# Attention and maxout FFN: pairs 14 to 31 turned by transposing DMAs between SBUF tiles, three requests moved in the opening

## The chip, the cores and the metric

The kernel runs on one core of a Trainium2 chip, as one program in one launch. The metric is the device time of an execution in microseconds (us). Five engines work on their own lists of instructions and wait for one another by semaphores: PE (TensorE, matmuls and transposes; its weight loads are shown apart as PEld), DVE (VectorE), ACT (ScalarE), POOL (GpSimd) and SP (SyncE, which here only issues DMAs). Sixteen DMA engines move the data. All times from the trace are counted from the first instruction of the profiled execution.

## The reference, cut to what matters

Attention runs per batch b (8) and head h (8) over 576 queries of width 64, with 16 beacon keys and values put before the 576 ordinary ones. The beacons are seen by all queries; the rest is causal. The result, 4608 tokens of 512, goes through a feed-forward layer with three first matrices, of which the maximum is taken, and one last matrix.

```python
k_all = np.concatenate([beacon_k, k], axis=2)
v_all = np.concatenate([beacon_v, v], axis=2)
scores = scale * np.matmul(q, k_all.transpose(0, 1, 3, 2))
scores = np.where(causal, -1000000000.0, scores)
a = np.exp(scores - scores.max(-1, keepdims=True))
a /= a.sum(-1, keepdims=True) + 1e-09
attn_out = np.matmul(a, v_all)                       # [B, H, S, D]
x = attn_out.transpose(0, 2, 1, 3).reshape(B * S, H * D)
h = np.maximum(np.maximum(x @ w1, x @ w2), x @ w3)   # 4608 x 768
out = h @ w_out                                      # 4608 x 512
```

Inputs and output are float32; the kernel computes in bf16 with float32 sums.

## The kernel before

**Pairs.** Two heads of one batch make a pair: 32 pairs, four to a batch. Pair p works in query tile qT (128 partitions: two heads of 64, 576 columns) and key tile kT (592 columns: 16 beacons, 576 keys), of which there are six each (`NT`), used in turn: p % 6. Two pairs make a block (`quad` in the code), and the main loop (L1140) handles blocks 4 to 15, that is pairs 8 to 31. The first eight pairs run in an opening that is written out as a list of steps (`first_steps`, L892).

**What a block does.** Scores of the first pair (`emit_scores`, L506: PE multiplies kT by qT into PSUM, ACT takes the exponential into `at_sb`, L532); the product with the values for the block before (`emit_pv`, L571, L592), its normalization on ACT and DVE (L612 to L624); then the rest of the scores, with POOL masking the causal edge (`emit_masks`, L538, L551). Between these stand units of the feed-forward layer (`mm1_unit`, L643 and L654, with DVE keeping the running maximum in hT, L664; `mm2_unit`, L685 and L690, with DVE's copy to y, L702). How many units stand at each of the six places of a block is set by hand in `gaps` (L1084). Once the attention is finished, at some 245 us, only feed-forward units remain.

**How q and k come into qT and kT.** `load_pair` (L192) loads a pair's q and k into a float32 staging tile, 96 partitions with six consecutive rows each, so that one piece of a row in DRAM is 6 x 64 x 4 = 1536 bytes. There are eight staging tiles, shared with the values, and a load follows the cast that frees one. `cast_pair` (L254, L248) casts it into the bf16 tile p, on POOL or ACT, with both heads side by side: 96 partitions x 6 rows x 128. From there two ways lead on:

- Pairs 4 to 15 are turned by PE (`turn_pair`, L472): six transposes for q and six for k (L401) into one tile of a ring of three PSUM tiles, then a copy of the keys on DVE (L467) and of the queries on ACT (L456), which put the columns into order.
- Pairs 16 to 31 are stored to DRAM (`store_pair`, L371) and fetched from there with a transposing DMA (`fetch_pair`, L380, L382 and L383). Their beacons are stored next to the keys in DRAM (`open_dram`, L362), so that one fetch brings both.

The beacons of batches 0 to 3 are turned by PE into `bT` and copied by ACT or POOL into the first 16 columns of kT (`place_beacons`, L461, L463).

**What sets the order.** Each engine runs its list in the order in which the program emits it. All loads, stores and fetches of the loop are issued by SP, in order: `at_step` (L773, L1068 to L1081) hangs them on steps (pair, first or second half). Pair p is cast at step p-5, stored at p-4 and fetched at p-3. An instruction at the head of a queue that waits holds all behind it. A DMA also waits for the one eight places ahead of it in SP's queue, whose semaphore it reuses. In the opening, some loads are gated: a memset of a few elements on DVE or POOL (L198, L283, L332) writes the target first, and the DMA waits for it, which sets when it may start. `load_w_out` (L330) does so for the last matrix, through POOL's DMA queue.

Of the kernel before, what the change touches and what calls it, by code (L numbers as in the profile page):

```python
# [8 lines left out]
FP32 = mybir.dt.float32  # L9
BF16 = mybir.dt.bfloat16  # L10
# [6 lines left out]
def kernel(  # L17
# [46 lines left out]

    B_PE = 4


# [52 lines left out]
    pv_psum = ctx.enter_context(tc.tile_pool(name="pv_psum", bufs=1, space=PSUM))  # L120
    dram_pool = ctx.enter_context(tc.tile_pool(name="dram", bufs=B - B_PE, space=bass.MemoryType.DRAM))
    ffn_stack = ctx.enter_context(ExitStack())
# [6 lines left out]
    NB_DMA = Nb * (B - B_PE)  # L129
    bT = const.tile([128, PPB, NB_PE], BF16, name="bT")  # L130
    bk32_0 = const.tile([Nb, H, D], FP32, name="bk32_0")
# [60 lines left out]
    def load_pair(p, gate=None):  # L192
        b, g, j0 = place(p)
        hs = slice(head(g, j0), head(g, j0) + 2)
        st = new_stage(("pair", p))

        if gate:
            gate.memset(st[0:QP, 0:1], 0.0)  # L198
        for i, src in enumerate((q, k)):
            nc.sync.dma_start(  # L200
                out=st[0:QP, i * NQ2 : (i + 1) * NQ2].rearrange("p (h x) -> p h x", h=2),
                in_=src[b, hs].rearrange("h (p r) d -> p h (r d)", r=QR),
            )

# [153 lines left out]

    q_dram = {}
    k_dram = {}  # L360

    def open_dram(b):  # L362
        q_dram[b] = dram_pool.tile([PPB, S, 2 * D], BF16, name="q_dram")
        k_dram[b] = dram_pool.tile([PPB, NK, 2 * D], BF16, name="k_dram")
        lo = Nb * (b - B_PE)
        nc.sync.dma_start(
            out=k_dram[b][:, 0:Nb].rearrange("i n x -> n i x"),
            in_=bk16[lo : lo + Nb].rearrange("n (i h) d -> n i (h d)", h=2),
        )

    def store_pair(p):  # L371
        b, pi = divmod(p, PPB)
        for i, dst in enumerate((q_dram[b][pi], k_dram[b][pi, Nb:NK])):
            src = stage.pop(("pair16", p, i))
            nc.sync.dma_start(
                out=dst.rearrange("(p r) x -> p (r x)", r=QR),
                in_=src.rearrange("p r h d -> p (r h d)"),
            )

    def fetch_pair(p):  # L380
        b, pi = divmod(p, PPB)
        nc.sync.dma_start_transpose(out=qTs[p % NT], in_=q_dram[b][pi])  # L382
        nc.sync.dma_start_transpose(out=kTs[p % NT][:, 0:NK], in_=k_dram[b][pi])  # L383

# [383 lines left out]

    plan = {}

    def at_step(p, g, *fns):  # L773
        plan.setdefault((p, g), []).extend(fns)

    def load_v_pieces(b):
# [11 lines left out]
    def next_load(n=1, gate=None):  # L788
        for _ in range(n):
            if loads:  # L790
                loads.pop(0)(*([idle[gate]] if gate else []))

    def C(fn, *a):
        def run():
            fn(*a)
            next_load()

        return run

# [48 lines left out]
    def widen():  # L848
        ffn_stack.close()
        wide = ctx.enter_context(tc.tile_pool(name="wide_psum", bufs=1, space=PSUM))  # L850
        ring.append((wide, "wide"))

    by = {"dve": by_dve, "act": by_act, "pool": by_pool}
    queue = {"sp": nc.sync, "act": nc.scalar}
# [34 lines left out]
        "load": next_load,  # L889
        "store": lambda: store_y(len(y_out)),  # L890
    }
# [108 lines left out]
        ("scores", 5, 0, 1),  # L1000
        ("scores", 4, 0, 0),
        ("scores", 4, 3, 0),
        ("ffn", "pv", 1),
        ("ffn", "ring", 0),
        ("load pair", 8, "dve"),
        ("ffn", "pv", 1),
        ("scores", 5, 3, 0),
        ("mask", 5, 0, "dve"),
        ("mask", 4, 2, "dve"),
        ("mask", 5, 3, "dve"),  # L1010
        ("load pair", 9, "pool"),
        ("scores", 5, 2, 0),
# [16 lines left out]
        ("mask", 5, 1, "pool"),  # L1029
        ("scores", 6, 0, 0),  # L1030
        ("ffn", "pv", 1),
        ("load", 1),
# [3 lines left out]
        ("cast pair", 8),  # L1036
        ("load w_out", "dve"),
        ("whole", 7, "ring"),
# [28 lines left out]
    ]  # L1067
    for p in range(10, B_PE * PPB):  # L1068
        at_step(p - 2, 0, C(cast_pair, p, by_pool, by_pool))
    for b in range(2, B):  # L1070
        p = b * PPB
        at_step(p + 1, 0, C(cast_v, b, 0, by_pool))
        at_step(p + 1, 1, C(cast_v, b, 1, by_pool))
    at_step(B_PE * PPB - 6, 1, L(by_pool, bk16, bk32))
    for b in range(B_PE, B):
        p = b * PPB
        at_step(p - 4, 0, L(open_dram, b))
        for i in range(PPB):
            at_step(p + i - 5, 0, C(cast_pair, p + i, by_act if b < 6 else by_pool, by_pool))
            at_step(p + i - 4, 0, L(store_pair, p + i))  # L1080
            at_step(p + i - 3, 0, L(fetch_pair, p + i))  # L1081


    gaps = {  # L1084
        4: (3, 2, 2, 3, 2, 1),
        5: (3, 1, 1, 3, 1, 1),
        6: (3, 1, 2, 0, 2, 1),
        7: (5, 1, 1, 1, 1, 0),
        8: (2, 3, 2, 7, 0, 2),
        9: (5, 1, 1, 1, 2, 0),  # L1090
        10: (2, 1, 2, 5, 2, 1),
        11: (3, 1, 1, 1, 2, 0),
        12: (2, 1, 2, 9, 0, 1),
        13: (5, 1, 1, 1, 0, 2),
        14: (2, 1, 2, 9, 2, 0),
        15: (4, 2, 1, 5, 2, 5),
    }

    def emit_all():
        for name, *args in first_steps:  # L1100
            steps[name](*args)
        n_y = 0

        def run_plan(p, s):
            for fn in plan.pop((p, s), ()):
                fn()

        def stored():
            nonlocal n_y
            store_y(n_y)  # L1110
            n_y = len(y_out)

        v_tiles.pop(0)
        early_stack.close()
        y_pool.append(ctx.enter_context(tc.tile_pool(name="ffn_y", bufs=4)))

        def singles(n):
            for _ in range(n):
                emit_ffn(END, single)

        def double():
            emit_ffn(END, next_tile, 2)

        def ffn_run(n):
            for _ in range(n // 2):
                double()
            singles(n % 2)

        def burst(*groups_):
            for x in groups_:  # L1130
                emit_scores(*x)
            for x in groups_:
                emit_masks(*x)

        def turn_next(p):
            if p < B_PE * PPB:
                turn_pair(p, by_act)
                place_beacons(p, by_act)

        for quad in range(2 * n_quad, NPAIR // PPQ):  # L1140
            pa, pb = PPQ * quad, PPQ * quad + 1
            if done[0] % 2:
                singles(1)
            at_single[0] = 0
            emit_scores(pa, 1)
            emit_scores(pa, 0)
            exp = emit_scores(pa, 2, now=False)
            emit_pv(quad - 1, 0)
            invert_sums()
            exp()  # L1150
            x = next_tile()
            emit_pv(quad - 1, 1, banks=[x[:, 0], x[:, 1]])
            for gi in (1, 0, 2):
                emit_masks(pa, gi)
            multiply()
            invert_sums()
            multiply()
            units_at = gaps[quad]
            ffn_run(units_at[0])
            stored()  # L1160
            run_plan(pa, 0)
            singles(units_at[1])

            burst((pa, 3), (pb, 0), (pb, 1))
            singles(units_at[2])
            stored()
            run_plan(pa, 1)
            turn_next(pa + PPQ)
            ffn_run(units_at[3])
            run_plan(pb, 0)  # L1170

            burst((pb, 2), (pb, 3))
            singles(units_at[4])
            turn_next(pb + PPQ)
            if quad == NPAIR // PPQ - 1:
                ffn_run(2)
            singles(units_at[5] - (2 if quad == NPAIR // PPQ - 1 else 0))
            stored()
            run_plan(pb, 1)
            if quad % n_quad == 0:  # L1180
                v_tiles.pop(quad // n_quad - 1)
        assert not plan and not loads
        double()
        emit_pv(NPAIR // PPQ - 1, 0)
        invert_sums()
        x = next_tile()
        emit_pv(NPAIR // PPQ - 1, 1, banks=[x[:, 0], x[:, 1]])
        multiply()
        invert_sums()
        multiply()  # L1190
        double()
        store_y(len(y_out))
        alone[0] = True
        last_mm1 = END - 4
        while done[0] < END - 1:
            turn_over = done[0] % UPB in (UPB - 6, UPB - 5)
            if done[0] >= last_mm1 or turn_over or not emit_ffn(END, next_tile, 2):
                emit_ffn(END, lambda: next_tile()[:, 0])
            store_y(len(y_out))
        mm2_last(n_tokb - 1, TOKB // 128 - 1, (0, 320, 512))  # L1200
# [33 lines left out]
```

## Time and profile before

| | |
|---|---|
| median of 3 runs | 294.12 us (293.96 to 294.83) |
| the profiled execution | 294.65 us |
| its span, first to last instruction | 292.6 us |
| granted TensorE clock | 1.0 |
| data moved by DMA | 49.50 MB, mean 169 GB/s |
| SP's queue (q1) | 78864 packets, 43.40 MB, 66.6% of the sixteen engines' span |

The profiled execution's time holds about 2 us that lie outside its span. An engine's idle time costs something only where another engine waits for it; the DMA packets' share is the time that the packets took, so that a share near or over 1 says that the sixteen engines had packets under way all the time. How the busy times lie in the span is shown below, where they are used.

### The profile page before, as it was taken

What the parts mean: (1) busy time and instruction counts of PE and PEld (TensorE: products, weight loads), DVE (VectorE), ACT (ScalarE), POOL (GpSimd) and SP (SyncE); (2) the same over time, 40 slices, a digit from 0 to 9 for tenths busy, and PEclk for the clock granted to TensorE, in tenths of its full rate; (3) what the DMA queues carried; (4) which work ended last, traced back from release to release, by engine and by line L of the source; (5) the groups of instructions that cost most, each with busy time, mean ns of one, the idle gap of its engine ahead of it and who ended that gap; (6) DMA issues with size and microseconds to landing.
All of it is one profiled execution on the core that took longest, in us unless ns stands there. A gap on an engine that the chain in (4) does not pass through costs nothing.

```text
span 292.6 us, 8864 instructions
## 1 busy us (share of the span) xinstructions
PE 281.3 (96%) x3714; PEld 160.1 (55%) x3739; DVE 169.6 (58%) x319; ACT 150.5 (51%) x242; POOL 115.8 (40%) x238
## 2 busy tenths in 40 slices
PE   8889999989999999999999999999999999999995
PEld 4656677754454555454545887545454545444442
DVE  1555567837756575566655656565656564474273
ACT  3786576853566676846676256635663552200300
POOL 3618415742546583426454655466323420000000
PEclk9999999999999999999999999999999999999999
DMA  7999979999989999998999899999442003001103
GB/s 131 161 175 185 217 123 225 228 192 261 229 230 256 232 281 270 186 175 263 314 190 181 233 256 268 177 205 214 104 68 98 2 0 137 11 0 74 71 1 143
DMA packets 85111, 49.50 MB, mean 169 GB/s; under 512 B 64208, under 2 KB 79824, under 8 KB 85072
## 3 DMA queue, kind: packets, MB, share of 16 engines
q1 hardware_dynamic: 78864, 43.40, 66.6%
q0 software_dynamic: 5648, 5.21, 11.7%
q8 instruction: 29, 0.48, 0.7%
q10 hardware_dynamic: 560, 0.33, 0.4%
q14 instruction: 10, 0.08, 0.1%
HBM read 35.13 MB, written 14.22 MB: 169 GB/s over the span
## 4 chain that ended last, share of the span: by engine, by line
PE 86%; DMA 7%; POOL 2%; ACT 2%; DVE 1%; issue 1%; POOLq 0%
PE pv L654 21%; PE sc L654 15%; PE wide L654 8%; PE pv L690 6%; PE sc L690 6%; PE sc L517 5%; PE pv L592 4%; DMA w_out_sb<-in_moe_w_out_dram 4%; PE wide L690 3%; PE wide L592 3%; PE sc L592 3%; PE wide L517 3%; DMA w_sb<-in_moe_w_dram 3%; PE pv L481 2%; PE pv L673 1%
## 5 line engine op out<-in xcount | busy, mean ns | idle before, releaser
L532 ACT ACTIVATE at_sb<-sc 128x736 bf16<-128x736 f32 (+5 forms) x91 | 76.5, 867 | 59.3 <-PE sc L517 59.1
L551 POOL TENSOR_SCALAR_AFFINE_SELECT at_sb<-at_sb 128x256 bf16<-128x256 bf16 (+3 forms) x140 | 51.9, 387 | 117.3 <-ACT at_sb L532 117.1
L654 PEld LDWEIGHTS <-w_sb 128*128 128x128 bf16 x648 | 61.1, 98 | 60.4 <-issue 4.7
L654 PE MATMUL pv<-xT,w_sb 128*128 128x512 bf16 (+1 forms) x315 | 65.3, 347 | 0.3
L654 PE MATMUL sc<-xT,w_sb 128*128 128x512 bf16 (+1 forms) x205 | 45.6, 363 | 0.7 <-issue 0.2
L532 ACT ACTIVATE at_sb<-wide 128x736 bf16<-128x736 f32 (+3 forms) x37 | 31.3, 846 | 22.4 <-PE wide L517 22.4
L664 DVE TENSOR_TENSOR hT<-hT,pv 128x512 bf16<-128x512 bf16 x48 | 32.4, 686 | 13.0 <-PE pv L654 13.0
L690 PEld LDWEIGHTS <-hT 128*128 128x128 bf16 x210 | 19.6, 98 | 24.3 <-issue 1.1
L248 POOL CAST p<-st 96x768 bf16<-96x768 f32 x40 | 32.0, 824 | 0.0
L624 DVE TENSOR_TENSOR xT<-pv,recip 128x288 bf16<-128x288 f32 (+2 forms) x48 | 14.2, 350 | 26.7 <-ACT recip L614 26.7
L517 PE MATMUL sc<-qT,kT 64*128 64x288 bf16 (+6 forms) x290 | 27.2, 275 | 2.0 <-POOL at_sb L551 0.6
L664 DVE TENSOR_TENSOR hT<-hT,sc 128x1024 bf16<-128x1024 bf16 (+1 forms) x18 | 19.6, 1098 | 12.7 <-PE sc L654 12.5
L517 PEld LDWEIGHTS <-kT 64*128 64x128 bf16 x400 | 14.9, 94 | 21.8 <-issue 14.7
L592 PEld LDWEIGHTS <-v_sb 128*32 128x32 bf16 (+1 forms) x1408 | 24.7, 96 | 2.6 <-issue 1.3
L654 PE MATMUL wide<-xT,w_sb 128*128 128x512 bf16 (+1 forms) x110 | 24.5, 364 | 0.1
L690 PE MATMUL sc<-w_out_sb,hT 128*128 128x512 bf16 x79 | 19.1, 380 | 1.0 <-DMA w_out_sb<-in_moe_w_out_dram 0.7
L690 PE MATMUL pv<-w_out_sb,hT 128*128 128x512 bf16 x83 | 19.9, 380 | 0.1
L304 POOL CAST v_sb<-st 128x1536 bf16<-128x1536 f32 (+2 forms) x21 | 18.4, 895 | 0.0
L662 DVE CAST hT<-pv 128x512 bf16<-128x512 f32 x20 | 13.7, 688 | 4.8 <-PE pv L654 4.8
L673 PEld LDWEIGHTS <-w_sb 128*128 128x128 bf16 x144 | 13.1, 98 | 3.9 <-issue 1.4
L614 ACT ACTIVATE recip<-lnd 128x288 f32<-128x288 f32 x32 | 14.2, 444 | 1.0
L592 PEld LDWEIGHTS <-ones 128*32 128x32 bf16 (+2 forms) x512 | 11.0, 95 | 6.7 <-issue 4.7
(116 smaller groups left out, 286.3 us busy)
## 6 DMA issues: line engine op xcount, KB each, us to landing
st<-in_q_dram SPq DMA_DIRECT2D x24, 288.0 KB, 5.3
st<-in_k_dram SPq DMA_DIRECT2D x24, 288.0 KB, 5.7
st<-in_v_dram SPq DMA_DIRECT2D x24, 256.0 KB, 5.8
out_dram<-y SPq DMA_DIRECT2D x9, 512.0 KB, 3.3
out_dram<-y SPq DMA_DIRECT2D x17, 256.0 KB, 2.7
w_sb<-in_moe_w_dram POOLq DMA_DIRECT2D x6, 384.0 KB, 7.2
q_dram<-p SPq DMA_DIRECT2D x16, 144.0 KB, 3.1
k_dram<-p SPq DMA_DIRECT2D x16, 144.0 KB, 3.2
```

The costliest lines, as they stand in the source:

```text
L248: cast(t16.rearrange("p r h d -> p h r d"), st[0:QP, i * NQ2 : (i + 1) * NQ2].rearrange("p (h r d) -> p h r d", h=2, r=QR),)
L304: cast(v_sb[0:n, t:t1].rearrange("p t h d -> p (t h d)"), st[0:n, (t - t_lo) * H * D : (t1 - t_lo) * H * D],)
L517: nc.tensor.matmul(ps[:, e, off : off + q1 - q0], kT[hs, 128 * t : 128 * t + 128], qT[hs, q0:q1], start=True, stop=True, tile_position=(64 ...
L532: nc.scalar.activation(out=both_heads(p, gi), in_=ps[:, :, 0 : g_width(p, gi)], func=AF.Exp, scale=scale)
L551: nc.gpsimd.affine_select(out=view, in_=view, compare_op=ALU.is_ge, fill=0.0, base=x0, pattern=[[0, 2], [1, hi - lo]], channel_multiplier=-1,)
L592: nc.tensor.matmul(ps[bank][32 * j : 32 * j + 32, lo + q0 - qa : lo + qb - qa], lhsT, at_view(PPQ * quad + j // 2, t, j % 2, q0, qb), star ...
L614: nc.scalar.activation(out=recip, in_=lnd, func=AF.Exp, scale=-1.0)
L624: nc.vector.tensor_mul(xT[:, 2 * g + part - 1, c0 + ca : c0 + cb], ps[bank][:, lo : lo + cb - ca], recip[:, ca:cb],)
L654: nc.tensor.matmul(dst[:, o0 : o0 + n], w_in[i][:, ct, 128 * (ft + f) : 128 * (ft + f + 1)], xT[:, ct, x0 : x0 + n], start=(ct == 0), stop ...
L664: nc.vector.tensor_max(h, h, ps)
L673: nc.tensor.matmul(ps[:, f], w_in[i][:, ct, 128 * (ft + f) : 128 * (ft + f + 1)], xT[:, ct, tb * TOKB + lo : tb * TOKB + hi], start=(ct == 0),
L690: nc.tensor.matmul(ps[:, t - tt] if two else ps, hT[:, ft, 128 * t : 128 * (t + 1)], w_out_sb[:, ft, :], start=(ft == 0), stop=(ft == n_ft ...
```

## The change

Pairs 14 to 31 (`P_X = 14`) go neither through PE nor through DRAM. A transposing DMA reads tile p in SBUF, 96 partitions x 768, and writes the six pieces of 128 x 96 columns into qT or kT (`cross_piece`). For the columns to come out in order, row r of a partition must be 96 rows from the next, and so their loads read `(r p)` in place of `(p r)`: rows of 64 floats, 256 bytes, in place of 1536. The beacons of batches 4 to 7 are turned once, by one transposing DMA between SBUF tiles (`cross_beacons`), and copied by ACT into each kT, as for the other batches. The DRAM tiles, the stores and the fetches go.

The loop over blocks, `at_step` and `gaps` are replaced by a written list (`loop_steps`), of which a part is shown. PE's instructions in it are those of before in the same order, but for the transposes of pairs 14 and 15 (2 x 12). Casts that ACT did (eight) are done by POOL. The transposes of an even pair stand where its fetch stood, those of an odd pair about half a block sooner.

In the opening, the loads of pairs 8 and 9 and that of w_out are moved up by a few steps. For pair 8 that moves the gate on DVE ahead of two instructions; pair 9 keeps its place on POOL and on SP. For w_out it moves the gate on DVE ahead of one instruction and the request on POOL ahead of the two casts of pair 8.

```diff
+    P_X = 14
...
-    bT = const.tile([128, PPB, NB_PE], BF16, name="bT")
+    bT = const.tile([128, PPB, Nb * B], BF16, name="bT")
...
         for i, src in enumerate((q, k)):
-            nc.sync.dma_start(
-                out=st[0:QP, i * NQ2 : (i + 1) * NQ2].rearrange("p (h x) -> p h x", h=2),
-                in_=src[b, hs].rearrange("h (p r) d -> p h (r d)", r=QR),
-            )
+            dst = st[0:QP, i * NQ2 : (i + 1) * NQ2]
+            if p < P_X:
+                nc.sync.dma_start(
+                    out=dst.rearrange("p (h x) -> p h x", h=2),
+                    in_=src[b, hs].rearrange("h (p r) d -> p h (r d)", r=QR),
+                )
+            else:
+                nc.sync.dma_start(
+                    out=dst.rearrange("p (h r d) -> p h r d", h=2, r=QR),
+                    in_=src[b, hs].rearrange("h (r p) d -> p h r d", r=QR),
+                )
...
+    def cross_beacons():
+        nc.sync.dma_start_transpose(
+            out=bT[:, :, Nb * B_PE : Nb * B], in_=bk16.rearrange("n h d -> n (h d)")
+        )
...
+    def cross_piece(p, i):
+        src = stage.pop(("pair16", p, i))
+        x0 = i * Nb
+        nc.sync.dma_start_transpose(
+            out=(qTs, kTs)[i][p % NT][:, x0 : x0 + S].rearrange("d (r p) -> d r p", r=QR),
+            in_=src.rearrange("p r h d -> p (r h d)"),
+        )
...
         ("scores", 4, 0, 0),
+        ("load pair", 8, "dve"),
         ("scores", 4, 3, 0),
         ("ffn", "pv", 1),
         ("ffn", "ring", 0),
-        ("load pair", 8, "dve"),
         ("ffn", "pv", 1),
         ("scores", 5, 3, 0),
+        ("load pair", 9, "pool"),
...
         ("scores", 6, 0, 0),
+        ("load w_out", "dve"),
         ("ffn", "pv", 1),
...
         ("cast pair", 8),
-        ("load w_out", "dve"),
...
-    for b in range(B_PE, B):
-        p = b * PPB
-        at_step(p - 4, 0, L(open_dram, b))
-        for i in range(PPB):
-            at_step(p + i - 5, 0, C(cast_pair, p + i, by_act if b < 6 else by_pool, by_pool))
-            at_step(p + i - 4, 0, L(store_pair, p + i))
-            at_step(p + i - 3, 0, L(fetch_pair, p + i))
...
+        ("cast", 14, "pool", "pool"),
+        ("load", 1),
...
+        ("cast keys 2", "pool"),
+        ("cross", 14, 0),
+        ("cross", 14, 1),
+        ("keys", 14, "act"),
+        ("cast", 15, "pool", "pool"),
+        ("load", 1),
...
+        ("cross keys",),
+        ("cross", 15, 0),
+        ("cross", 15, 1),
+        ("keys", 15, "act"),
```

More of the change, by code (lines that the diff above doesn't have):

```diff
@@ L120 @@
     pv_psum = ctx.enter_context(tc.tile_pool(name="pv_psum", bufs=1, space=PSUM))
-    dram_pool = ctx.enter_context(tc.tile_pool(name="dram", bufs=B - B_PE, space=bass.MemoryType.DRAM))
     ffn_stack = ctx.enter_context(ExitStack())
@@ L355, in turn_beacons @@
         by_act(bT[:, :, Nb * b0 : Nb * b1], ps)
[L359 to L368, printed above, removed]
-        )
[L371 to L383, printed above, removed]
+    def cross_beacons():
+        nc.sync.dma_start_transpose(
+            out=bT[:, :, Nb * B_PE : Nb * B], in_=bk16.rearrange("n h d -> n (h d)")
+        )
+    def cross_piece(p, i):
[5 more added lines that the diff above has]
+        )
     def turn(p, i, ps):
@@ L767, in emit_ffn @@
         return False
-    plan = {}
-    def at_step(p, g, *fns):
-        plan.setdefault((p, g), []).extend(fns)
     def load_v_pieces(b):
@@ L791, in next_load @@
                 loads.pop(0)(*([idle[gate]] if gate else []))
[L793 to L798, printed above, removed]
     def make_tri():
@@ L851, in widen, with wait_exp, ffn_next, start_late @@
         ring.append((wide, "wide"))
+    waiting = {}
+    def wait_exp(p, gi):
+        waiting[p, gi] = emit_scores(p, gi, now=False)
+    def ffn_next(n, bank):
+        get = {"ring": next_tile if n == 2 else lambda: next_tile()[:, 0]}
+        for i in range(2):
+            get[f"pv{i}"] = lambda i=i: pv_bank(i, [128, 512], FP32)
+        assert emit_ffn(END, get[bank], n)
+    def start_late():
+        early_stack.close()
+        y_pool.append(ctx.enter_context(tc.tile_pool(name="ffn_y", bufs=4)))
     by = {"dve": by_dve, "act": by_act, "pool": by_pool}
@@ L889 @@
         "load": next_load,
-        "store": lambda: store_y(len(y_out)),
+        "store": lambda n=0: store_y(n or len(y_out)),
+        "late": start_late,
+        "score": wait_exp,
+        "exp": lambda p, gi: waiting.pop((p, gi))(),
+        "cross": cross_piece,
+        "pair": lambda p, e: turn_pair(p, by[e]),
+        "cross keys": cross_beacons,
+        "ffn 1": lambda bank: ffn_next(1, bank),
+        "ffn 2": lambda: ffn_next(2, "ring"),
+        "cast": lambda p, qe, ke: cast_pair(p, by[qe], by[ke]),
+        "cast keys 2": lambda e: by[e](bk16, bk32),
     }
@@ L1010 @@
         ("mask", 5, 3, "dve"),
-        ("load pair", 9, "pool"),
         ("scores", 5, 2, 0),
@@ L1067 @@
     ]
-    for p in range(10, B_PE * PPB):
-        at_step(p - 2, 0, C(cast_pair, p, by_pool, by_pool))
-    for b in range(2, B):
-        p = b * PPB
-        at_step(p + 1, 0, C(cast_v, b, 0, by_pool))
-        at_step(p + 1, 1, C(cast_v, b, 1, by_pool))
-    at_step(B_PE * PPB - 6, 1, L(by_pool, bk16, bk32))
-    for b in range(B_PE, B):
-        p = b * PPB
-        at_step(p - 4, 0, L(open_dram, b))
-        for i in range(PPB):
-            at_step(p + i - 5, 0, C(cast_pair, p + i, by_act if b < 6 else by_pool, by_pool))
-            at_step(p + i - 4, 0, L(store_pair, p + i))
-            at_step(p + i - 3, 0, L(fetch_pair, p + i))
@@ L1099, in emit_all @@
     def emit_all():
-        for name, *args in first_steps:
+        for name, *args in first_steps + loop_steps:
             steps[name](*args)
[L1102 to L1181, printed above, removed]
@@ L1182, in emit_all @@
-        assert not plan and not loads
-        double()
+        assert not loads and not stage
         emit_pv(NPAIR // PPQ - 1, 0)
@@ L1190, in emit_all @@
         multiply()
-        double()
+        emit_ffn(END, next_tile, 2)
         store_y(len(y_out))
```

535 lines of the change are left out of this document (521 added, 14 removed).

## The prediction

> **What bounds the kernel now.** I read the page first: busy times, then the slices, then what the engines waited for, the chain, and the DMA issues.
>
> ```profile
> PE 281.3 (96%) x3714; PEld 160.1 (55%) x3739; DVE 169.6 (58%) x319; ACT 150.5 (51%) x242; POOL 115.8 (40%) x238
> ...
> DMA  7999979999989999998999899999442003001103
> ```
>
> TensorE (PE) is busy for 281.3 of 292.6 us. The sixteen DMA engines are as full, up to slice 28 (some 205 us), and nearly idle afterwards. Which of the two sets the end is told by PE's waits. Over the whole span, and then for 66 to 250 us alone (engine, line, waited for: us in total, times, longest):
>
> ```profile
> PE sc L690 <- DMA w_out_sb<-in_moe_w_out_dram: 0.7, 1, 0.7
> ...
> PE sc L654 <- issue: 0.2, 1, 0.2
> ```
>
> The last line is the only one that the second answer gives. So from 66 us on PE waits for nothing: the DMA engines are full but in time, and the end moves only if PE's own list gets shorter, if a wait before 66 us goes, or if something new makes PE wait. The chain of waits, asked for 58 to 64 us and for 103 to 110 us (start, us, what), shows the two places that the change touches:
>
> ```profile
> 50.77 12.37 DMA w_out_sb<-in_moe_w_out_dram
> ...
> 104.27 0.51 PE sc L401 x12
> ...
> 107.06 0.51 PE sc L401 x12
> ```
>
> The first is the transfer of w_out, requested at 50.77 and landed at 63.14, for which PE stood 0.7 us. The others are the TensorE transposes of pairs 14 and 15, twelve each.
>
> **Part 1: PE's list.** PE's instructions in the changed kernel are those of before in the same order, less 24 transposes and their 24 weight loads (two of the three PSUM ring tiles swap names after that). Both groups lie on the chain: 2 x 0.51 = **-1.02 us**. The two key copies on DVE (0.75 us each) and query copies on ACT (0.64 each) that go with them were off it: nothing.
>
> **Part 2: w_out, pairs 8 and 9.** The request of w_out waits on POOL for a one-element memset on DVE (L332). It stood behind the running maximum of 49.76 and ran at 50.39; now it stands behind that of 47.84, so it runs at about 48.5. POOL is free then (its cast of the values ends at 47.1, a mask at 47.4). The request is some 2.1 us earlier. Ahead of it, the gate of pair 8's load moves from after the maximum of 42.54 to after the cast of 39.59, from 43.17 to about 40.3, so the SP queue with pairs 8 and 9 and the values behind them starts 2.9 us earlier, on DMA engines that in the slice before were nearly empty. With the same 12.37 us to landing w_out is there at 61.0, and PE wants it at 62.45 (63.18 less the 0.73 that it stood): **-0.73 us**, with 1.4 us to spare. If only 0.7 us of the 2.1 came through, the wait would still be gone. Next late after it is nothing: the same matmuls need hT, whose last maximum ended at 52.8. The price is on POOL: the two casts of pair 8 (0.82 us each), which ran at 47.35, now follow the request's 0.84 us and end at about 51.1. PE turns pair 8 at 52.97, so nothing; without that margin, each us late would be a us of PE. The mask behind them (51.61 before) starts at about the same time.
>
> **Part 3: POOL, ACT and DVE in the loop.** POOL takes eight casts (L248, 0.82 us) from ACT, 6.6 us in all. It stands idle before its masks for 117 us in sum; a mask behind a pair's casts is late by 1.6 us at most, and PE waits for no mask after 66 us: nothing. ACT loses 8 x 0.82 + 2 x 0.64 and gains sixteen beacon copies of 0.21 us (L463): 4.5 us less, nothing. One of these copies, pair 16's, waits for the beacons' own transposing DMA, and behind it on ACT stands the exp of pair 13's next group (107.07 before). The store of beacons in that place of the SP queue was issued at 99.10; with the 4 to 6 us to landing of a fetch the copy is free at 103 to 105, and the exp is due at about 105.3: nothing, and 1 us if the transfer is slow.
>
> **Part 4: the DMA engines and the SP queue.** This is where the change can go wrong. Issues of before (out<-in, KB each, median us to landing):
>
> ```profile
> q_dram<-p SPq DMA_DIRECT2D x16, 144.0 KB, 3.1
> k_dram<-p SPq DMA_DIRECT2D x16, 144.0 KB, 3.2
> ...
> qT<-q_dram SPq DMA_TRANSPOSE x16, 4.8
> kT<-k_dram SPq DMA_TRANSPOSE x16, 4.2
> ```
>
> The 32 stores go. The 32 fetches become 36 transposes that read the cast tile p in SBUF, and one for beacons. The loads of pairs 14 to 31 come in rows of 256 bytes instead of 1536. Rates from the table by stage (PE, PEld, DVE, ACT, POOL busy; clock; DMA share; GB/s): the first stretch holds loads in 1536-byte rows and outputs, the second mostly values in 256-byte rows:
>
> ```profile
> 85.30:95.00 9.70, 9.65 (x83) 4.68 (x83) 6.96 (x10) 6.34 (x11) 5.11 (x10) 1.00 1.03 260
> ...
> 122.00:124.00 2.00, 2.00 (x72) 1.37 (x74) 0.83 (x2) 1.72 (x3) 0.89 (x3) 1.00 1.25 219
> ```
>
> Stores: 32 x 0.147 MB at 260 GB/s, 0.57 us each, -18.1 us of DMA time. Loads: 0.295 MB takes 1.13 us at 260 and 1.35 at 219, 36 x 0.21 = +7.7. Four more transposes and the beacons' at 0.147 MB / 219 = 0.67 us: +3. Sum -7 us, if a transpose from SBUF costs what one from DRAM does.
>
> No row shows that. Both halves are shown: reading tile p (the store, 0.57 us) and writing qT through the transposing path (the fetch, 0.67). Lower bound 0.57, as if only the reading counted; upper bound 1.24, as if the halves ran one after the other. I take 0.67, since the fetch shares the kind of instruction and the writing side. What PE allows is read from the tightest even pair, 24 (even pairs keep their place in the program, odd ones move half a block forward): its keys' fetch, issued at 167.82, landed at 173.2, and its scores start at 181.3: 8 us. Twenty-two transposes are issued by then; DMA time saved and added cancel within 1 us there, and one store trip of 3.1 us falls out of the chain from load to use. So (8 + 3.1) / 22 = 0.5 us more is hidden, **up to 1.17 us each**; beyond, every 0.1 us costs 2.2 us. At the upper bound this is +1.5 us.
>
> The issue on the SP queue: a fetch occupies it for 1.13 to 2.32 us, median 1.21 (L382, L383). A block of two pairs takes 15.0 us (pair 16's scores at 122.2, pair 30's at 227.1, seven blocks). Four loads at 0.45, some three pieces of values at 0.5 and two outputs at 0.4 leave 10.8 us for four transposes: **2.7 us each** are hidden. I take 1.2; lower end 1.13; upper end 6 x 1.13 = 6.8, since the new form writes six pieces of 96 columns and could be issued as six. The row it is nearest to is the fetch: one instruction, the same 576 rows.
>
> **Sum.** -1.02 - 0.73 = **-1.75 us**. The profiled execution took 294.65 us, 292.6 of it span; its sum is 292.9. It lay 0.53 above the median of the runs, 294.12, so by the median **292.4 us**, a span of 290.9.
>
> **The rivals.**
>
> A, slower by DMA time. If a transpose from SBUF takes over 1.17 us of the DMA engines, scores wait for kT from pair 20 on. At 2.0 us: 22 x 0.83 = 18 us late, 310 us; at 1.4, 5 us, 297. For it: the engines are full already, and only 96 partitions are read. Against: the store reads the same tile in 0.57. Chance 0.10.
>
> B, slower by issue: the SP queue pushes the six pieces one by one. Above 2.7 us each it decides. At 6.8 us a block needs 27 + 4.2 = 31 us where PE needs 15; nine blocks x 16 us less the 8 of margin: about +136, 430 us. For it: even the plain fetch takes three times a load's issue. Against: it is still one instruction. [...] No transpose from SBUF is in this trace. Chance 0.12.
>
> C, no change: PE's saved time returns as waits before 66 us, for the late cast of pair 8 or the held exp of pair 13: 293.3 to 295. Chance 0.08. Against: the margins of 1.9 and 1 us above.
>
> D, a mixture of small waits after 66 us, 295 to 297: 0.04.
>
> **How the numbers follow.** Forecast 0.66. A measurement of this kernel can tell about 0.3%, 0.9 us, from no change: faster is below 293.24, slower above 295.0. Faster 0.68 (the forecast, and C where only the transposes count, 293.1), same 0.06, slower 0.26 (A, B, D and a little). Low end 291.5: the forecast less one more stall of the opening (0.56 before L592 at 60.6) and measuring error. High end 298: it takes in C, D, the 1.24 us bound and the lower part of A; left out are the rest of A, 0.06, and B, 0.12.
>
> **What would show it.** Right: PE waits neither for w_out nor, after 66 us, for ACT, POOL or DMA; L401 has 24 fewer; transposes issue in 1 to 2.5 us; pair 24's keys land some us before their scores. Wrong: PE's weight loads or scores waiting for DMA kT or ACT's copies, holes in PE's slices from 120 us on, an SP queue whose transposes last over 2.7 us, or DMA engines full well beyond 205 us.

## The result, and the profile after

The changed kernel takes 293.24 us (median of 20 runs, 292.38 to 294.96); the kernel before, run beside it, 294.06 us (20 runs, 293.49 to 294.83). The ratio is 0.9971, with a 95% interval of 0.9958 to 0.9983: faster by 0.8 us. Run again beside the experiments it gave 0.9966 (0.9945 to 0.9987). The forecast was 292.4. The time lies just at the 293.24 below which the prediction called a result faster; that it is faster at all is told by the interval, which leaves out 1.

The profiled execution of the changed kernel is one of its slower ones (294.61 us, span 292.6), the same as that of before. So the two profiles show what was gained, and also what an unlucky execution loses. From its page:

```profile
PE 279.6 (96%) x3690; PEld 158.7 (54%) x3715; DVE 168.4 (58%) x317; ACT 145.2 (50%) x248; POOL 121.4 (41%) x246
...
DMA  7999999999989979999999999999852003001103
...
q1 hardware_dynamic: 111984, 39.20, 71.4%
...
q8 instruction: 29, 0.48, 0.7%
```

PE has 24 matmuls and 24 weight loads less, ACT 5 us less, POOL 6 us more. The DMA engines are full about as long as before. SP's queue moves 4 MB less, yet its packets (42% more of them) take 71.4% of the span and no longer 66.6%. The last line, 29 packets of together 0.48 MB, I had passed over; it comes back below. What PE waited for, over the whole span (engine, line, waited for: us in total, times, longest; matmuls with w_out are now L682, the half units of the feed-forward layer L665, their maximum L675, masks L543, value sums L584, casts L255):

```profile
PE pv L665 <- DVE hT L675: 1.4, 1, 1.4
...
PE fps L665 <- DMA w_sb<-in_moe_w_dram: 1.3, 1, 1.3
...
PE pv L584 <- POOL at_sb L543: 0.2, 1, 0.2
PE sc L584 <- issue: 0.2, 1, 0.2
```

The wait for w_out is gone. In its place stand a wait of 1.4 us for DVE's maximum, which before did not exist, and 0.2 us for a mask after 66 us, where PE had waited for nothing. The second line is a transfer at 29 us, where the two kernels are alike (0.6 us in the profile of before, none to 1.2 in those of the experiments).

A table by stage says where the time lies. A stage runs from one block's value sums to another's on PE, in us, from the traces:

| stage (about) | before | changed | changed, again |
|---|---|---|---|
| B: 54 to 80 us, end of the opening | 25.91 | 26.23 | 25.78 |
| C: 95 to 109 us, block with pairs 14, 15 turned by PE | 14.92 | 13.92 | 13.92 |
| D: 170 to 181 us | 11.33 | 11.33 | 12.65 |
| E: 198 to 211 us | 12.98 | 13.75 | 12.98 |

Stage C gives the 1.0 us of the transposes. Stage B should have given the 0.73 us of w_out and gives about nothing. D and E lose 1.3 or 0.8 us in one execution and nothing in another. The experiments go through these four.

### The profile page after: what moved, and what is told of

Its sections match the earlier page's. It is cut to its first block, busy times and chain, and to the rows that moved or that the text cites. A ratio compares the mean times of both kernels' runs of the same rounds, so it can differ in the third digit from the quotient of the medians.

```text
span 292.6 us, 8805 instructions
## 1 busy us (share of the span) xinstructions
PE 279.6 (96%) x3690; PEld 158.7 (54%) x3715; DVE 168.4 (58%) x317; ACT 145.2 (50%) x248; POOL 121.4 (41%) x246
## 3 DMA queue, kind: packets, MB, share of 16 engines
q1 hardware_dynamic: 111984, 39.20, 71.4%
## 4 chain that ended last, share of the span: by engine, by line
PE 82%; DMA 6%; ACT 3%; POOL 3%; DVE 2%; issue 2%; ACTq 0%; POOLq 0%
PE pv L646 20%; PE sc L646 13%; PE wide L646 8%; PE sc L682 8%; PE sc L584 7%; PE pv L682 6%; PE sc L509 5%; PE pv L584 5%; DMA w_sb<-in_moe_w_dram 3%; PE wide L509 3%; DMA qT<-p 2%; PE pv L665 2%; DMA bk<-in_beacon_k_dram 1%; PE wide L682 1%; ACT at_sb L524 1%
## 5 line engine op out<-in xcount | busy, mean ns | idle before, releaser
L524 ACT ACTIVATE at_sb<-sc 128x736 bf16<-128x736 f32 (+5 forms) x87 | 72.8, 863 | 63.7 <-PE sc L509 63.0
L543 POOL TENSOR_SCALAR_AFFINE_SELECT at_sb<-at_sb 128x256 bf16<-128x256 bf16 (+3 forms) x140 | 51.4, 385 | 103.6 <-ACT at_sb L524 103.4
L524 ACT ACTIVATE at_sb<-wide 128x672 bf16<-128x672 f32 (+3 forms) x41 | 35.1, 857 | 22.9 <-PE wide L509 22.7
L646 PE MATMUL sc<-xT,w_sb 128*128 128x512 bf16 (+1 forms) x202 | 44.1, 362 | 0.3
L255 POOL CAST p<-st 96x768 bf16<-96x768 f32 x48 | 38.0, 822 | 9.3 <-DMA qT<-p 6.9
L682 PEld LDWEIGHTS <-hT 128*128 128x128 bf16 x210 | 19.6, 98 | 23.5 <-issue 1.1
L646 PE MATMUL wide<-xT,w_sb 128*128 128x512 bf16 (+1 forms) x113 | 26.1, 364 | 0.5 <-issue 0.2
L584 PEld LDWEIGHTS <-v_sb 128*32 128x32 bf16 (+1 forms) x1408 | 24.7, 96 | 1.6 <-issue 0.4
L682 PE MATMUL sc<-w_out_sb,hT 128*128 128x512 bf16 x103 | 24.4, 379 | 0.3
L656 DVE TENSOR_TENSOR hT<-hT,sc 128x1024 bf16<-128x1024 bf16 (+1 forms) x15 | 17.0, 1147 | 5.6 <-PE sc L646 5.5
L682 PE MATMUL pv<-w_out_sb,hT 128*128 128x512 bf16 x83 | 19.9, 380 | 0.1
L656 DVE TENSOR_TENSOR hT<-hT,wide 128x1024 bf16<-128x1024 bf16 (+1 forms) x11 | 12.3, 1121 | 10.8 <-PE wide L646 10.6
L665 PEld LDWEIGHTS <-w_sb 128*128 128x128 bf16 x144 | 13.1, 97 | 6.1 <-issue 2.9
L616 DVE TENSOR_TENSOR xT<-sc,recip 128x288 bf16<-128x288 f32 (+2 forms) x39 | 11.5, 351 | 7.9 <-ACT recip L606 7.9
```

Source lines behind the costliest of these rows:

```text
L255: cast(t16.rearrange("p r h d -> p h r d"), st[0:QP, i * NQ2 : (i + 1) * NQ2].rearrange("p (h r d) -> p h r d", h=2, r=QR),)
L524: nc.scalar.activation(out=both_heads(p, gi), in_=ps[:, :, 0 : g_width(p, gi)], func=AF.Exp, scale=scale)
L543: nc.gpsimd.affine_select(out=view, in_=view, compare_op=ALU.is_ge, fill=0.0, base=x0, pattern=[[0, 2], [1, hi - lo]], channel_multiplier=-1,)
L584: nc.tensor.matmul(ps[bank][32 * j : 32 * j + 32, lo + q0 - qa : lo + qb - qa], lhsT, at_view(PPQ * quad + j // 2, t, j % 2, q0, qb), star ...
L616: nc.vector.tensor_mul(xT[:, 2 * g + part - 1, c0 + ca : c0 + cb], ps[bank][:, lo : lo + cb - ca], recip[:, ca:cb],)
L646: nc.tensor.matmul(dst[:, o0 : o0 + n], w_in[i][:, ct, 128 * (ft + f) : 128 * (ft + f + 1)], xT[:, ct, x0 : x0 + n], start=(ct == 0), stop ...
```

## The experiments

All differences to before are of medians measured beside each other.

### Stage B: a bank, the early requests, and what stands behind them

In the opening's last step a unit of the feed-forward layer lies in PSUM bank pv0 (the seventh of those that take pv0 and pv1 in turn). The kernel before went on with pv1; the written list names pv0 again. PE writes it only after DVE's maximum has read it, and stands 1.36 us for that. The chain of waits of the changed kernel (start, us, what) shows the loop: PE's value sums, ACT's reciprocal, DVE's multiplication, then the maximum, then PE.

```profile
56.32 0.42 ACT lnd L604
...
58.23 0.51 DVE xT L616 x2
58.74 0.61 DVE hT L675
59.34 0.04 issue
59.39 1.05 PE pv L665 x8
```

**e1_bank**: the other bank.

```diff
         ("late",),
-        ("ffn 1", "pv0"),
+        ("ffn 1", "pv1"),
```

> The changed kernel, with the loop's first FFN unit in PSUM bank pv1 instead of pv0; the opening's last unit sits in pv0. Theory 1: in the changed kernel TensorE waits at 57.9 us for VectorE's maximum to read pv0 (1.36 us in the profile: PE pv L665 <- DVE hT L675 1.4), because the change names pv0 where the kernel before alternated and came to pv1. With pv1 the wait goes: 1.3 us under the changed kernel's 293.2, about 291.9, ratio to before 0.993. Rival 1: that wait belongs to the profiled execution alone (TensorE had paused 0.43 us just before); then 293.2, ratio 0.997. Rival 2: the wait before the value sums at 60.1 us in the kernel before (0.56 us) comes back: 292.5, ratio 0.995.

292.93 us, ratio 0.9953 (0.9931 to 0.9975): 1.4 us under before, which is what rival 2 said (0.995) and short of theory 1 (0.993). The wait for DVE is gone from its profile. But the units that now run 1.4 us sooner bring PE only to another stop a microsecond later, of 1.03 us. PE's timeline in e1_bank (start, us, engine, line, operation; in brackets the idle time before and what ended it):

```profile
59.54 0.52 PE L584 MATMUL pv<-at_sb,v_sb 128*32 128x288 bf16 x19
61.09 0.30 PE L584 MATMUL pv<-at_sb,v_sb 128*32 128x80 bf16 x12 [1.03 <-issue]
```

The stop is in the middle of a run of matmuls, at one that waits for no semaphore. The kernel before stops at the same matmul for 0.56 us, which I had listed as one stall of the opening and not looked into:

```profile
60.63 0.29 PE L592 MATMUL pv<-at_sb,v_sb 128*32 128x80 bf16 x12 [0.56 <-issue]
```

**e9_shift**: e1_bank with 64 tiny instructions more in PE's warm-up (`tiny`: 32 weight loads, each with a matmul of 8 columns).

```diff
         ("busy", 17),
+        ("tiny", 32),
```

> As e1_bank, with 64 tiny instructions more on TensorE (32 weight loads and 32 matmuls of 8 columns) in its warm-up. Theory: the stop of 1.03 us that e1_bank has instead of the bank's wait is TensorE waiting for its own program: it stands at TensorE's instruction 1985, others at 1729, which is 256 earlier, and it ends 1.3 to 1.6 us after a 16,384-byte instruction DMA has landed. Then it stays at 1985 by count, and so moves 64 instructions back in the code, from the middle of pair block 3's value sums into the scores of pair 7 ahead of them. Rival: it is a wait of that place in the code (a bank, a mask, the values' cast): then it stays at the 20th matmul of the value sums, instruction 2049 by count.

One execution, 293.29 us. The stop has moved out of the value sums (now L591) into the scores (L516):

```profile
58.96 0.36 PE L516 MATMUL wide<-qT,kT 64*128 64x464 bf16 x1
59.67 0.37 PE L516 MATMUL wide<-qT,kT 64*128 64x464 bf16 x1 [0.36 <-issue]
59.97 0.41 PE L591 MATMUL pv<-at_sb,ones 128*32 128x288 bf16 x12
60.21 0.62 PE L591 MATMUL pv<-at_sb,v_sb 128*32 128x288 bf16 x32
```

By count (all of PE's recorded instructions, from 0) it is again PE's instruction 1985, and at 2049, where the code of the old place now lies, PE does not stop. So PE waits for its own program. The 29 packets of queue q8 have 16,384 bytes each, and PE's 7,431 recorded instructions make 29 blocks of 256. Stops like this one lie at counts of 193 + 256n (1985 above all, also 1729 and 5057); there are 23 in the 14 traces where over 0.35 us lie from the start of one instruction to the start of the next, and each ends 1.31 to 1.64 us after such a packet has landed. At 1985 the packet begins to move when PE is only 37 to 83 instructions short of the place, at a time when the DMA queues are full (a busy share of 1.08 over 51.2 to 65.8 us in the kernel before, 1.18 in the changed one). In the opening PE passes 256 short instructions in 5.4 us (1729 to 1985, in the kernel before); in the twelve profiles with the stop, 1985 runs only 5.9 to 6.6 us after 1729. PE lost 0.4 to 1.2 us at 1985 in every profile but the two of the changed kernel.

Those two lose it as well, under another name: while PE waits for the bank, the packet lands (in the first profile at 60.2 us; PE reaches instruction 1985 at 61.8). With the bank free PE would have stood there until 1.3 to 1.6 us after the landing, 61.5 to 61.8. So by this estimate the bank costs 0 to 0.3 us in that execution, 0.2 to 0.5 in the other, and not the 1.4 that its wait shows. The times cannot separate so little, and no run shows it: 0.9953 against 0.9971 and 0.9966, with intervals that overlap.

With the stops named, stage B adds up to within 0.2 us. The next kernel, e3_opening_only, takes 25.02 us there and has one stop, of 0.47, which leaves 24.55 us of work. Before: 24.55 + 0.56 + 0.73 (w_out) makes 25.84 of its 25.91. The changed kernel: 24.55 + 1.36 (the bank) + 0.24 (a stop at 1729) makes 26.15 of its 26.23, and 24.55 + 1.36 makes 25.91 of the 25.78 of the other execution.

**e3_opening_only**: the kernel before with the opening's list of the changed one (the three moved requests of the diff, nothing else).

> The kernel before, with only the requests of pairs 8 and 9 and of w_out moved as in the change. My prediction's sum: the w_out wait of 0.73 us goes, nothing comes instead: 293.3, ratio 0.9975; with the 0.56 us wait at 60.1 us gone as well, 292.8, ratio 0.9956. Rival: the saved wait comes back before 66 us (a late cast of pair 8, the exp of pair 13 behind it): ratio 1.000.

293.68 us, ratio 0.9974 (0.9954 to 0.9994), 0.6 us under before, as my sum said; stage B takes 25.02 us, 0.89 less, with the w_out wait gone. The term of 0.73 us holds where nothing else fills the place.

**e13_wout_back**: only w_out's request at its old place, on the kernel e6_keys_early (next part).

```diff
-        ("load w_out", "dve"),
         ("ffn", "pv", 1),
...
         ("cast pair", 8),
+        ("load w_out", "dve"),
```

> As e6_keys_early, with only w_out's request back at its old place; pairs 8 and 9 stay early. Theory (my prediction's term): w_out lands some 2 us later, at about 62.5 to 63, where TensorE wants it at 61.7 to 62.7: 0.3 to 1 us above e6_keys_early, with a wait of the matmul with w_out in the profile. Rival: the gain of the early requests is that SP as a whole runs ahead, and pairs 8 and 9 bring that: equal to e6_keys_early.

292.89 us, ratio 0.9962 (0.9939 to 0.9985), against 0.9951 of e6_keys_early; both 1.06 us under before. My theory fell: the request was issued 2.3 us later (50.55 against 48.23) and landed at about the same time (60.6 against 60.4), and PE did not wait. The kernel before requested it at 50.77, only 0.2 us later still, and there it landed at 63.14. So by these profiles, one of each kernel, what makes w_out early is that the loads of pairs 8 and 9 go ahead of it sooner.

### Stage C: the transposes, and the copy that waits for the beacons

**e5_px16**: e1_bank with pairs 14 and 15 as before, on PE (the same edit for 15; their casts and turnings stand where the kernel before had them).

```diff
-    P_X = 14
+    P_X = 16
...
-        ("cross", 14, 0),
-        ("cross", 14, 1),
...
+        ("pair", 14, "act"),
```

> As e1_bank, but pairs 14 and 15 are loaded, cast and turned by TensorE where the kernel before did it; pairs 16 to 31 and the beacons cross by DMA. My prediction's sum: 2 x 0.51 us more on TensorE and nothing else, so 1.0 us above e1_bank, ratio 0.9965 if e1_bank is at 0.993. Rival: those two pairs' transposes were hidden or their crossing pays elsewhere (DMA and SP busier, casts of later pairs held): equal to e1_bank or below it.

294.03 us, ratio 0.9994 (0.9972 to 1.0017): 1.1 us above e1_bank on the same chip, 0.94 in stage C of the profiles (14.86 against 13.92). The term of 1.02 us is right, and the rival fell.

**e2_loop_only**: e1_bank with the opening's requests at their old places, so the loop's change alone.

> As e1_bank, with the requests of pairs 8 and 9 and of w_out back at their old places in the opening; so the turning of pairs 14 to 31 alone. My prediction's sum: 24 transposes less on TensorE, 1.02 us, so before minus 1.0 = 293.0, ratio 0.9965, and 0.7 us above e1_bank (the w_out wait of 0.73 us is back). If the early requests bring nothing: equal to e1_bank, ratio 0.993. If the transposes leave TensorE but the time comes back as masks held behind late casts on POOL: ratio 1.000.

295.82 us, ratio 1.0036 (1.0010 to 1.0062): slower than before, which none of the three lines expected. Stage C takes 15.78 us. ACT and PE in its timeline:

```profile
109.65 0.20 ACT L455 COPY kT<-bT 128x16 bf16<-128x16 bf16 x1 [4.39 <-DMA bT<-bk]
109.76 0.94 ACT L524 ACTIVATE at_sb<-sc 128x928 bf16<-128x928 f32 x1
110.59 0.72 ACT L524 ACTIVATE at_sb<-wide 128x672 bf16<-128x672 f32 x1
```

```profile
110.74 0.39 PE L509 MATMUL sc<-qT,kT 64*128 64x288 bf16 x4 [1.27 <-ACT at_sb L524]
```

ACT stands 4.4 us at the copy of pair 16's beacons, which needs their transposing DMA; the exps behind it are late, and PE, which needs their PSUM tile, stands 1.3 us. That DMA was issued at 105.3 us here, at 103.1 in the changed kernel (ACT waits 2.4 us, PE not at all), at 100.6 in e1_bank (0.4). The late requests of the opening may be part of what puts SP behind here, 50 us later, but no run shows how much. The changed kernel and e1_bank, which have the same opening, differ by 2.5 us as well. And in the profiled execution of e2_loop_only the granted clock was 0.66 over 20 to 25 us (1.00 in that of e7_loop_keys, below), so that all of it lies later. The clock does not explain the slower median: the nine of its twelve executions at 0.998 or more have one of 295.2 us.

**e6_keys_early** and **e7_loop_keys**: e1_bank and e2_loop_only with the beacons' DMA right behind its cast.

```diff
         ("cast keys 2", "pool"),
+        ("cross keys",),
         ("cross", 14, 0),
...
-        ("cross keys",),
```

> As e1_bank, with the beacons' transposing DMA moved ahead of pair 14's two, right behind the cast it needs. Theory: ScalarE's copy of pair 16's beacons, which stands ahead of exps, waits for that DMA (0.4 us in the profile of e1_bank, 2.4 in that of the changed kernel, 4.4 in that of e2_loop_only, where TensorE then lost 1.3 us to the exp); here the DMA lands some 10 us sooner and ScalarE waits for it no more. In e1_bank's own profile TensorE loses nothing by it, so the median moves only by the executions in which it is later: 0 to 0.5 us under e1_bank, ratio 0.9935 to 0.9955. Rival: pair 14's two transposes, now one place later, come late for its scores: over 0.9955.

> As e2_loop_only (opening's requests at their old places), with the beacons' transposing DMA early as in e6_keys_early. Theory: e2_loop_only was slower than before (1.0036) because its SP queue ran 2 us later, the beacons landed late and the exps behind the copy on ScalarE held TensorE; with the beacons early the transposes' 1.0 us shows and the early requests are worth the w_out wait alone: ratio 0.9965 to 0.9985, and 0.5 to 1.2 us above e6_keys_early. Rival: e2_loop_only was slow by the granted clock (0.994 in its profile) or by something else in the opening: it stays at 1.002 or more.

e6_keys_early: 292.66 us, ratio 0.9951 (0.9930 to 0.9973), not to be told from e1_bank. e7_loop_keys: 293.52 us, 0.9997 (0.9972 to 1.0021), stage C 13.91 us, and no wait of ACT for the beacons in either profile. So the beacons made e2_loop_only slower: the wait is gone and the ratio falls from 1.0036 to 0.9997, though the two intervals overlap a little. With them mended the early requests are worth 0.86 us (293.52 to 292.66), near their 0.73. But e7_loop_keys shows no wait for w_out in its profile: the difference to e6_keys_early stands there as a longer stop at 1985 (1.2 us against 0.6), so that the near agreement is in part luck. That e7_loop_keys shows only 0.2 of the transposes' 1.0 us in its median goes with what its profile has: 1.2 us of stop at 1985 (0.56 before) and 0.96 us in stage E.

**e8_px12**: e6_keys_early with pairs 12 and 13 by DMA as well (the same edit for 13, and their casts ahead of those of 14 and 15).

```diff
-    P_X = 14
+    P_X = 12
...
-        ("pair", 12, "act"),
+        ("cross", 12, 0),
+        ("cross", 12, 1),
```

> As e6_keys_early, with pairs 12 and 13 crossing by DMA as well (loaded in 256-byte rows, cast before pairs 14 and 15, no TensorE transposes). If a pair's transposes are worth what e5_px16 against e1_bank showed (1.10 us for two pairs, 0.94 in the profiles): 1.0 us under e6_keys_early, ratio near 0.990. Rival: DMA and SP are by now so full that casts wait for transposes, masks for casts, and the gain is lost: ratio 0.994 or more.

300.19 us, ratio 1.0204 (1.0168 to 1.0240). The rival, and much beyond it: one pair's keys come too late for its scores.

```profile
PE sc L509 <- DMA kT<-p: 4.7, 1, 4.7
```

Its loads and casts at 84 to 97 us had no room left: POOL stood 5.9 us at a cast because a transpose still read the buffer, and the transposes of pairs 12 and 13 were issued between 93.0 and 98.7 us. Not all of the 7.5 us above e6_keys_early is waiting: the granted clock was 0.66 over 95 to 100 us, right behind this wait, and 0.989 to 0.994 over the six executions (0.998 to 1.0 in those of e6_keys_early). Pairs 14 and 15 are where the room for this method ends, without other changes.

### Stages D and E, and the DMA engines' time

In stage E of the changed kernel the chain goes through a cast that waits for a transpose (start, us, what):

```profile
189.57 5.18 DMA qT<-p
...
195.66 0.82 POOL p L255
196.48 1.41 POOL v_sb L311
197.89 0.73 POOL at_sb L543 x2
198.62 0.04 issue
198.66 0.38 PE pv L584 x7
```

There are three buffers for cast pieces. The cast of a new pair waits until the transpose of an older one has read its buffer (4.3 us at the longest in this profile), a cast of values follows, and two masks stand behind both; PE's value sums need the masks.

**e10_bufs4**: e6_keys_early with a fourth buffer (every fourth pair's pieces in a pool of their own).

```diff
-        t16 = pair_pool.tile([QP, QR, 2, D], BF16, name=f"p16{i}")
+        pool = pair_late[0] if pair_late and p % 4 == 1 else pair_pool
+        t16 = pool.tile([QP, QR, 2, D], BF16, name=f"p16{i}")
```

> As e6_keys_early, with a fourth buffer for the cast pieces from pair 13 on (pairs 13, 17, 21, 25 and 29 in a buffer of their own). Theory: casts on POOL wait for the transposing DMAs that still read the buffer (7 to 12 us in all, 4.3 at a time), and masks stand behind the casts; in the profile of the changed kernel that cost TensorE 0.77 us between 181 and 197 us. With the buffer these waits all but go, and TensorE waits for no mask: 0.2 to 0.6 us under e6_keys_early, and fewer executions above 294. Rival: e6_keys_early loses nothing there: equal.

292.69 us, ratio 0.9956 (0.9927 to 0.9985). The mechanism is as thought: the waits of POOL's casts for transposes, some 10 us in e6_keys_early, are gone, and stage E is 12.98 us (13.42 in e6_keys_early). The time is not lower: it fits the rival. This profile loses 0.75 us in stage D instead, with a stop of 0.55 us for the program (see e12_after_again).

**e11_rows1536**: the loads of pairs 14 to 31 in long rows.

```diff
-            if p < P_X:
+            if True:
```

> As e6_keys_early, with pairs 14 to 31 loaded in rows of 1,536 bytes as in the kernel before; the columns of their turned queries and keys then stand in another order than the masks, so the scores of these pairs are of other tokens. It prices the 256-byte rows: by the packets of the profiles, 34,560 more packets cost some 29 us of 16 DMA engines' time. Theory: with them gone the DMA queues shorten, SP runs ahead, casts wait for no transpose: 0.2 to 0.8 us under e6_keys_early. Rival: the DMA time is hidden altogether: equal.

292.55 us, ratio 0.9957 (0.9930 to 0.9983): again equal. The packets' time falls from 251.2 us of sixteen engines to 226.5. So the 256-byte rows cost some 24.7 us of DMA time, 0.69 us a load, and in the median the kernel does not feel it. This is one profile of each; nine profiles with the same transfers, that of e6_keys_early among them, lie between 241.1 and 254.8 us, so the price of a load is known only to some 0.4 to 0.8 us. This profile, too, has stage E at 12.98 and a stop in stage D.

**e12_after_again**: the changed kernel.

> The changed kernel once more, beside the others on one chip. Theory: ratio 0.997, and above e6_keys_early by the bank's wait less what the program's stop takes in its place (0.3 to 0.7 us). Its profile shows the wait for VectorE (1.2 to 1.5 us at 58 us) again, and no stop at instruction 1985. Rival: the wait was of that one profiled execution; then the profile shows the stop at 1985 in place of it.

293.02 us, ratio 0.9966 (0.9945 to 0.9987). Its profile shows the bank's wait again and none at 1985, and in stage D this:

```profile
PE pv L665 <- DVE hT L675: 1.4, 1, 1.4
...
PE sc L584 <- issue: 1.1, 1, 1.1
```

The second line is a stop for the program at instruction 5057, in the value sums of 171 us. The 48 instructions that left PE's list ahead of it moved the block's borders by nearly as many in the code: the block that ends there now holds almost only short instructions and is passed in 2.9 us (4801 to 5057 in the first profile of the changed kernel; 4.9 in that of before). Stops of 0.2, 0.6, 0.6 and 1.1 us at this place are in four of the later profiles; in the three kernels that keep the 48 instructions (before, e3_opening_only, e5_px16) stage D has none. That the shift is the cause fits this; no run tests it alone.

## Why the prediction was right, and by how much less

The direction and the range were right, and so was the larger term. The sum was 1.75 us, measured were 0.8 to 0.9, about half. That the time still lies in the range owes something to the range's width, 291.5 to 298, which was made for slower rivals that did not come.

- **Part 1, PE's list: right.** 1.02 us expected, 1.00 in stage C, 1.1 by e5_px16 against e1_bank.
- **Part 2, w_out: mechanism right, "next late after it is nothing" wrong.** Requested at 48.8 and landed at 61.5 us (expected 48.5 and 61.0), no wait; e3_opening_only gives the 0.6 us. In the changed kernel two things stood right behind. PE's list was the same in order, but I had compared operations and the ring's tiles, and not the pv banks, in which one unit now meets its predecessor. And the 0.56 us that I carried over from before as one more stall was a wait for the program; such waits ended 1.31 to 1.64 us after the packet had landed, and PE, which came to this one at 60.1 us in before and in e1_bank, stood 0.56 us in the one and 1.03 in the other. In the stage table the whole 0.73 us went there; the medians alone could not tell it from the scatter. This is the failed step. Rival C had such waits before 66 us return, but for pair 8's cast and pair 13's exp, and neither came. That the request's own place mattered was wrong as well, once pairs 8 and 9 are early (e13_wout_back).
- **Part 3, POOL: wrong in a detail that shows only in some executions.** "A mask behind a pair's casts is late by 1.6 us at most" counted the casts' time and not what they wait for: up to 4.3 us for a transpose that reads the buffer. It cost 0.8 us in one profile of the changed kernel, nothing in the other, and nothing that the medians of e10_bufs4 or e11_rows1536 could show.
- **Part 3, the beacons' copy: named, and tighter than I had it.** Free at 103 to 105 us expected, 107.0 found; PE lost nothing by it here, and 1.3 us in e2_loop_only.
- **Part 4, DMA time: hidden as said, with the wrong sign.** I had -7 us; the packets took 247.8 us of sixteen engines where those of before took 232.8, +15.0 (241.1 to 254.8 in the nine profiles with these transfers). The mis-sized term is the loads in 256-byte rows: +0.21 us each from the GB/s of two stages, 0.69 measured. Rates of stages mix kinds; the packets show means of 25 to 27 ns for 256 bytes and 89 to 108 for 1536.
- **Part 4, transposes and issue: rivals A and B did not come.** PE waits for no transpose; pair 24's keys landed at 177.2 us, 3.4 us before its scores at 180.6 (8 us in the kernel before). The issue on SP's queue (ns: least, median, most):

```profile
L374 SPq DMA_TRANSPOSE qT<-p x18: 1202/1982/3640, 91.7 to 212.1; - x18
L374 SPq DMA_TRANSPOSE kT<-p x18: 1213/1225/1687, 95.1 to 214.5; - x18
```

The keys' take what a fetch took (median 1.2 us in both); the queries', which come first, hold up to 3.6 us, over the 2.7 that I allowed, but not every time (median 2.0), so that SP kept up. None came near the 6.8 us of rival B.

What stays open: why the packets of the program come sooner or later from one execution to the next (the stop at 1985 lay between 0.4 and 1.2 us), and how much of the spread of the changed kernel's times (292.4 to 295.0) goes to them and how much to the casts. No run of mine parts these. Nor is e6_keys_early proved faster than the changed kernel: 0.9951 against 0.9966 and 0.9971, within each other's intervals. Both beat the kernel before.

## What to carry to other kernels

Ask of every wait that goes what stands within a microsecond behind it, and of a wait marked issue in the middle of a run of matmuls whether it lies a multiple of 256 instructions from another, as 1729, 1985 and 5057 do here: such a stop took back 1.03 us in e1_bank of the 1.36 saved ahead of it. When a schedule is written out by hand, compare the buffers that it names and not the operations alone. A transfer that leaves PE's list moves into the queues: look which copy or cast now stands in front of something that PE needs, for it failed here in executions in which the queues were late (in e2_loop_only ACT stood 4.4 us at the copy of pair 16's beacons, and PE 1.3 us behind it).

## What the runs showed of the hardware

- PE stopped at some of its 256th instructions (193 + 256n) for its own program, for up to 1.2 us (at 1985 in e7_loop_keys). Around 1985 the DMA queues were full: a busy share of 1.08 in the profile of before and 1.18 in that of the changed kernel. The 29 packets of its program come about one to each 256 instructions. Stops at 171 us appear only in kernels with 48 instructions fewer ahead of them.
- A transposing DMA from SBUF to SBUF (96 x 768, bf16) takes SP 1.2 to 3.6 us to issue and lands 2.5 to 6.1 us after it in the changed kernel; by the packet counts it makes 576 packets of 256 bytes, as the fetch from DRAM does. Packets of 256 bytes, of all kinds together, take 25 to 27 ns on average in the 14 traces.
- Six packets of 256 bytes cost about 160 ns of a DMA engine where one of 1536 costs 89 to 108: 1.5 to 1.8 times as much.
